# Decode attention beside a gated MLP on one core: weight matrices laid flat in 4.5 rows a partition, w_gate first, and half rows told apart in the sums over partitions

## The chip, the cores and the metric

The kernel runs on one core of a Trainium2 chip. The metric is the device time of one execution in microseconds (us), the median of several runs. All data are float32.

## The reference

One token is decoded: attention over a long cache, beside a gated MLP, both from the same normalised row x.

```python
D, H, Sk, Dh, Df = 576, 32, 16384, 128, 4608
xn = (x - mean(x)) / sqrt(var(x) + 1e-5)               # x: [576]
q  = (xn @ wq).reshape(H, Dh)                          # wq: [576, 4096]
s  = einsum("hd,hkd->hk", q, k_cache) * Dh**-0.5       # k_cache: [32, 16384, 128]
o  = einsum("hk,hkd->hd", softmax(s), v_cache)         # v_cache: [32, 16384, 128]
a  = o.reshape(4096) @ wo                              # wo: [4096, 576]
h  = gelu(xn @ w_gate) * (xn @ w_up)                   # both [576, 4608], gelu by tanh
out = x + a + h @ w_down                               # w_down: [4608, 576]
```

The caches are 537 MB of the 588 MB that are read; wq has 9.4 MB, w_gate and w_up 10.6 MB each.

## The kernel before

**What one head does.** The K cache of a head is one tile of 8.4 MB, 128 positions on each of 128 partitions, in two buffers that take turns (kb for even heads, ka for odd ones); V has one buffer, vt. DVE multiplies the whole K tile by q (qb, on every partition) and sums over the 128 features (L398, L402). TensorE and ScalarE make the softmax from that; TensorE multiplies the weights pe by V in 32 matmuls of 4 weight columns and 512 streamed columns (L386). Four of these stand in four different quarters of the array's columns. All large loads are issued on SP, one after the other, by an order written out by hand: before each, SP waits for a semaphore that says that the buffer is free.

**The three projections ahead of the heads.** `xn @ w` for wq, w_gate and w_up is made on DVE, because a row vector times a matrix needs every weight once. A matrix is laid with 4 of its first 512 rows on each partition (loads q0, q2 of wq, and so on), and the last 64 rows, cut into halves, make a tail with half a row on each partition (qt, gt, ut). `rows` scales each row on a partition by its element of xn (xp, xt) and adds them up: one tensor_scalar (L277) and scalar_tensor_tensor instructions (`add`, L266); the last ones write the tile both. What remains is the sum over the partitions. `sums` (L292 to L300) makes it on TensorE for each of the three matrices, with a weight tile of ones in 32 columns: the columns of both are cut into four quarters i and three banks b, and quarter i goes to the output partitions 32 i to 32 i + 31:

```python
m = g.matmul(pw[32 * i : 32 * i + 32, b, :SEL], ones[:, :32], bv[:, i, b * SEL : (b + 1) * SEL], start=True, stop=True)
```

`select` (L305 to L311) then turns the row of sums into a tile: a product with the mask m32 and a reduction on DVE. For q it makes qsel, from which TensorE and ScalarE make qb; for w_gate and w_up it makes gu (for w_up ScalarE and GpSimd do it). In the order on DVE, the select of a matrix stands between the rows of the next matrix, so that TensorE can sum meanwhile.

**What sets the order of the loads.** The buffers of the projections lie in the same memory as kb, ka and vt. wq and w_gate are loaded at once; w_up waits for the last row of wq; K of head 0 (two halves) for the last row of w_gate; K of head 1 for the third row of w_up (the semaphore value u_k); V of head 0 for the third sum (s_w, 3). After that each K load waits for s_kf (DVE is done with that buffer) and each V load for s_vf (TensorE is done with vt).

**The end.** w_down and wo are loaded last; DVE and TensorE share the sums of the last products.

Of the kernel before, what the change touches and what calls it, by code (L numbers as in the profile page):

```python
# [142 lines left out]
def plan(nc, pl, x, k_cache, v_cache, wq, wo, wg, wu, wd, out):  # L143
# [47 lines left out]
    qw, qt = [big("q0", 2 * HD, C + 8 * HD), big("q2", 2 * HD, C)], big("qt", HD // 2, C - 2 * HD)
    both = big("both", 12 * SEL, C + 8 * DF + 256)
    gw, gt = [big("g0", 2 * DF, B + 10240), big("g2", 2 * DF, A - 4 * DF)], big("gt", DF // 2, B)
    uw, ut = [big("u0", 2 * DF, A + 6 * DF), big("u2", 2 * DF, C)], big("ut", DF // 2, A + 4 * DF)
# [51 lines left out]
    k_xd = op("dve", lambda g: g.tensor_copy(xd, xn[:, DM:].unsqueeze(2).to_broadcast([1, D - DM, 2])), k_xn)
    xm = xn[:, :DM].rearrange("o (p j) -> o j p", j=DJ)
    for j in range(DJ):
        k = op("pe", lambda g, j=j: g.transpose(px[:, j : j + 1], xm[:, j, :], ones[:1, :1]), k_xn)
    k = op("pe", lambda g: g.transpose(px[:, DJ : DJ + 1], xd.rearrange("o d s -> o (d s)"), ones[:1, :1]), k_xd)  # L250
    k = op("dve", lambda g: g.tensor_copy(xp, px[:, : DJ + 1]), k)
    k_x = op("dve", lambda g: g.tensor_scalar(xt, par, xp[:, DJ:], None, op0=ALU.mult), k, c_par)
    c_h = op("dve", lambda g: g.tensor_copy(hcol[:, :H].rearrange("p (q r) -> p q r", q=4),
                                            ident.rearrange("p (q r) -> p q r", q=4)[:, :, : H // 4]), i1)
# [13 lines left out]
    def tails(s, t, d):  # L268
        n = t.shape[-1]
        for i in range(2):  # L270
            c = s[:, i * n : (i + 1) * n]
            add(c, t, xt[:, i : i + 1], c, d)

    def rows(w, t, d, parts, between=None):
        n = w[0].shape[-1] // 2
        r = [u[:, j * n : (j + 1) * n] for u in w for j in range(2)]
        op("dve", lambda g: g.tensor_scalar(r[0], r[0], xp[:, :1], None, op0=ALU.mult), d[0], k_x)  # L277
        add(r[1], r[1], xp[:, 1:2], r[0])
        made = between and between()
        for i in range(2):  # L280
            c = r[1][:, i * n // 2 : (i + 1) * n // 2]
            add(c, t, xt[:, i : i + 1], c, d[1])
        k_s = add(r[2], r[2], xp[:, 2:3], r[1], d[2])
        v = [u.rearrange("p (i c) -> p i c", i=4) for u in (r[3], r[2])]
        for lo, hi, to in parts:
            k = add(bv[:, :, to : to + hi - lo], v[0][:, :, lo:hi], xp[:, 3:4], v[1][:, :, lo:hi])
        pads = [op("pool", lambda g, lo=lo, hi=hi: g.memset(bv[:, :, lo:hi], 0.0), k_s)
                for lo, hi in ((384, SEL), (SEL + 384, 2 * SEL), (2 * SEL + 256, 3 * SEL)) if len(parts) > 1]
        pl.then("dve", [s_r], k, *pads[-1:])
        return k_s, k, made  # L290
# [13 lines left out]

    def select(dst, c, r, n):  # L305

        t = dst.shape[-1]
        v = sel[:, : 3 * c].rearrange("p (b r t) -> p b r t", b=3, t=t)
        m = m32[:, : 3 * c // t].rearrange("p (b r) -> p b r", b=3).unsqueeze(3).to_broadcast([P, 3, c // t, t])
        k = op("dve", lambda g: g.tensor_mul(v, pw[:, :, :c].rearrange("p b (r t) -> p b r t", t=t), m), (s_w, n), c_m32)  # L310
        return op("dve", lambda g: g.tensor_reduce(dst, sel[:, : r * t].rearrange("p (r t) -> p t r", r=r), axis=AX.X, op=ALU.add), k)  # L311
# [264 lines left out]
```

## Time and profile before

| | |
|---|---|
| median of 3 runs | 1361.17 us (1360.52 to 1361.29) |
| the profiled execution, its own time | 1361.59 us |
| its span, first to last instruction | 1360.3 us |
| DVE busy | 1243.2 us (91%) |
| TensorE matmuls busy (PE) | 389.3 us (29%) |
| ScalarE (ACT), GpSimd (POOL) busy | 66.8 and 35.9 us |
| read from HBM | 587.60 MB, 432 GB/s over the span |

Busy shares are means over the whole span. The head of the program, up to about 130 us, where the projections are made and the first heads are loaded, is told by the timeline and not by the shares. The trace shows each float32 matmul as two MATMULs, here called passes, so 12 matmuls of the program are 24 in it. Four passes that stand in different column quarters of the array overlap in time.

### The profile page before, as it was taken

What the parts mean: (1) busy time and instruction counts of PE and PEld (TensorE: products, weight loads), DVE (VectorE), ACT (ScalarE), POOL (GpSimd) and SP (SyncE); (2) the same over time, 40 slices, a digit from 0 to 9 for tenths busy, and PEclk for the clock granted to TensorE, in tenths of its full rate; (3) what the DMA queues carried; (4) which work ended last, traced back from release to release, by engine and by line L of the source; (5) the groups of instructions that cost most, each with busy time, mean ns of one, the idle gap of its engine ahead of it and who ended that gap; (6) DMA issues with size and microseconds to landing.
All of it is one profiled execution on the core that took longest, in us unless ns stands there. A gap on an engine that the chain in (4) does not pass through costs nothing. (4 is left out here: it accounts for less than half of the span.)

```text
span 1360.3 us, 6949 instructions
## 1 busy us (share of the span) xinstructions
PE 389.3 (29%) x2640; PEld 121.8 (9%) x2640; DVE 1243.2 (91%) x222; ACT 66.8 (5%) x234; POOL 35.9 (3%) x29
## 2 busy tenths in 40 slices
PE   0211233333221333333222333332223333322135
PEld 0000011011000111101000111000001111000011
DVE  7999999999988888899888888998888889988888
ACT  0000000000000000000000000000000000000000
POOL 0063000000000000000000000000000000000000
PEclk9655666666556666666556666665666666655667
DMA  9999999999999999999999999999999999999998
GB/s 404 429 438 432 432 432 432 447 443 436 432 432 432 432 432 432 432 432 432 443 447 436 432 432 432 432 432 432 432 432 432 437 453 436 432 432 432 431 428 378
DMA packets 12245, 587.62 MB, mean 432 GB/s; under 512 B 1362, under 2 KB 1618, under 8 KB 2132
## 3 DMA queue, kind: packets, MB, share of 16 engines
q1 hardware_dynamic: 12242, 587.60, 99.8%
q8 instruction: 1, 0.02, 0.0%
q10 hardware_dynamic: 2, 0.00, 0.0%
HBM read 587.60 MB, written 0.00 MB: 432 GB/s over the span
## 5 line engine op out<-in xcount | busy, mean ns | idle before, releaser
L386 PE MATMUL po<-vt,pe 128*4 128x512 f32 x2048 | 291.8, 733 | 605.7 <-PEq L130 605.7
L398 DVE TENSOR_TENSOR kb<-kb,qb 128x16384 f32<-128x16384 f32 (+1 forms) x17 | 277.3, 16314 | 31.9 <-DVEq L130 31.8
L398 DVE TENSOR_TENSOR ka<-ka,qb 128x16384 f32<-128x16384 f32 x16 | 275.6, 17225 | 31.4 <-DVEq L130 31.4
L402 DVE TENSOR_REDUCE sc<-kb 128x128 f32<-128x16384 f32 x16 | 275.5, 17220 | 2.3
L402 DVE TENSOR_REDUCE sc<-ka 128x128 f32<-128x16384 f32 x16 | 275.5, 17220 | 2.3
L386 PEld LDWEIGHTS po<-vt,pe 128*4 128x4 f32 x2048 | 56.4, 98 | 814.1 <-issue 814.1
L379 PE MATMUL pt<-ident,pm 128*1 128x128 f32 x32 | 11.9, 371 | 227.2 <-PEq L130 227.2
L437 ACT ACTIVATE o<-po 128x512 f32<-128x512 f32 x32 | 19.1, 597 | 871.4 <-ACTq L130 871.4
L391 PE MATMUL pc<-m,o 128*128 128x1 f32 x256 | 32.7, 249 | 28.9 <-PEq L130 28.9
L391 PEld LDWEIGHTS pc<-m,o 128*128 128x128 f32 x256 | 31.0, 191 | 57.8 <-issue 57.8
L266 DVE SCALAR_TENSOR_TENSOR wacc<-wd,hT,wacc 128x576 f32<-128x576 f32 x36 | 29.5, 819 | 4.1 <-DMA wd<-in_B_w_down_dram 2.9
L299 PE MATMUL pw<-both,ones 128*32 128x396 f32 x72 | 11.9, 826 | 62.5 <-PEq L130 62.5
L407 DVE TENSOR_REDUCE nm<-pt 1x1 f32<-1x128 f32 x32 | 8.9, 279 | 21.5 <-DVEq L130 21.5
L379 PEld LDWEIGHTS pt<-ident,pm 128*1 128x1 f32 x32 | 2.5, 79 | 232.4 <-issue 232.4
L381 PE MATMUL pb<-nm,ones 1*128 1x1 f32 x64 | 17.7, 343 | 18.5 <-PEq L130 18.5
L381 PEld LDWEIGHTS pb<-nm,ones 1*128 1x128 f32 x64 | 15.9, 306 | 27.9 <-issue 27.9
L433 ACT ACTIVATE nb<-pb 128x1 f32<-128x1 f32 x32 | 5.5, 172 | 258.3 <-ACTq L130 258.3
L405 DVE TENSOR_REDUCE pm<-sc 128x1 f32<-128x128 f32 x32 | 9.2, 286 | 7.6 <-DVEq L130 7.6
L377 PE MATMUL pqb<-qsel,hsel 128*128 128x128 f32 x64 | 15.3, 321 | 1.8 <-PEq L130 1.8
L435 ACT ACTIVATE pe<-sc,nb 128x128 f32<-128x128 f32 x32 | 12.8, 402 | 6.1 <-ACTq L130 6.1
L318 ACT ACTIVATE hsel<-hcol 128x128 f32 (+1 forms) x34 | 10.2, 301 | 40.5 <-DVE qsel L311 40.4
L340 POOL TENSOR_TENSOR tmp<-tmp 128x576 f32<-128x576 f32 (+3 forms) x4 | 11.3, 2835 | 0.3
(89 smaller groups left out, 173.7 us busy)
## 6 DMA issues: line engine op xcount, KB each, us to landing
g<-in_B_w_gate_dram SPq DMA_DIRECT2D x2, 4608.0 KB, 39.5
u<-in_B_w_up_dram SPq DMA_DIRECT2D x2, 4608.0 KB, 32.3
q<-in_A_wq_dram SPq DMA_DIRECT2D x2, 4096.0 KB, 17.4
kb<-in_A_k_cache_dram SPq DMA_DIRECT2D x2, 4096.0 KB, 25.8
wd<-in_B_w_down_dram SPq DMA_DIRECT2D x1, 8064.0 KB, 42.0
wo<-in_A_wo_dram SPq DMA_DIRECT2D x1, 3456.0 KB, 35.9
wd<-in_B_w_down_dram SPq DMA_DIRECT2D x1, 2304.0 KB, 28.1
wo<-in_A_wo_dram SPq DMA_DIRECT2D x1, 2304.0 KB, 40.9
```

Of the source, the lines that this page charges most:

```text
L266: return op("dve", lambda g: g.scalar_tensor_tensor(out, w, c, into, op0=ALU.mult, op1=ALU.add), *deps)
L299: m = g.matmul(pw[32 * i : 32 * i + 32, b, :SEL], ones[:, :32], bv[:, i, b * SEL : (b + 1) * SEL], start=True, stop=True)
L340: k = op("pool", lambda g, o=o, r=r: g.tensor_tensor(o, v[:, :r, :], v[:, r : 2 * r, :], op=ALU.add), k)
L377: g.matmul(pqb[:, 0, :DH], hsel, qsel, start=True, stop=True).then_inc(s_pq, 1)
L379: g.transpose(pt[:1, 0, :P], pm, ident).then_inc(s_pt, 1)
L381: g.matmul(pb[:, 0, :1], ones[:1, :], nm, start=True, stop=True).then_inc(s_pb, 1)
L386: m = g.matmul(po[q : q + 4, 0, :], pe[:, k : k + 4], vt[:, k * DH : (k + 4) * DH], start=k < 16, stop=k >= N - 16)
L391: m = g.matmul(pc[:, 0, :1], o4[:, j * DH : (j + 1) * DH], m32[:, j : j + 1], start=j == 0, stop=j == 3)
L398: g.tensor_mul(kd, kd, qb[i].unsqueeze(1).to_broadcast([P, n[1] - n[0], DH])).then_inc(s_d, 1)
L402: g.tensor_reduce(sc[i], kt[i].rearrange("p (n d) -> p n d", d=DH), axis=AX.X, op=ALU.add).then_inc(s_d, 1)
L435: g.activation(pe, sc[i], AF.Exp, bias=nb, scale=SCALE, accum_out=ls[:, bass.ds(h, 1)]).then_inc(s_p, 1)
L437: g.activation(o4, po[:, 0, :], AF.Copy).then_inc(s_o4, 1)
```

## The change

- The order of the matrices is w_gate, wq, w_up instead of wq, w_gate, w_up.
- Each matrix is laid flat: 1152 half rows, 9 on each partition (NK), all contiguous in HBM. There is no tail. A matrix comes in two loads: 5 and 4 half rows for w_gate, 4 and 5 for wq and w_up. Each matrix has one tile (g, q, u); u takes the place of g.
- `rows` goes by half rows. On an even partition the half rows with even k are first halves of a row, on an odd partition second halves. It keeps two running sums, one for even and one for odd k, and each writes half of both.
- So a sum over partitions must tell even partitions from odd ones. mk holds blocks of 32 columns, with ones on the even partitions, with ones on the odd ones, or with zeros, and each matmul now takes 128 weight columns out of it and adds into all 128 output partitions: four matmuls accumulate in each of three banks. Streamed columns are 384 instead of 396, and the padding of both is gone.
- xp gets 9 columns, made from a spread copy of xn (xd), five transposes and three DVE instructions.
- hcol, the mask m96 (for w_gate's select, which needs 12 columns a piece) and mk are made on POOL; po and acc are cleared on ACT instead of DVE.
- w_up waits for the last row of w_gate, K of head 0 for the last row of wq, K of head 1 for the last row of w_up. qb of head 0 is made after the second sum instead of the first.

```diff
-DJ = 4
-DM = P * DJ
+NK = 2 * D // P
-SEL = 396
+SEL = 384
...
     B, A, C = 0, SLOT, 2 * SLOT
...
+    AT = 2 * HD * NK
+    END = AT + 2 * DF * NK
+    qw, gw = big("q", HD * NK // 2, 0), big("g", DF * NK // 2, AT)
+    uw, both = big("u", DF * NK // 2, AT), big("both", 12 * SEL, END)
+    mk, m96 = big("mk", 256, END + 48 * SEL), big("m96", 96, END + 48 * SEL + 1024)
...
-    d_q = [dma("sp", qw[0], main["q"][:, : 2 * HD]), dma("sp", qt, tail["q"]), dma("sp", qw[1], main["q"][:, 2 * HD :])]
+    def halves(w):
+        return w.rearrange("d (s f) -> (d s) f", s=2).rearrange("(p k) f -> p (k f)", k=NK)
+
+    def load(t, w, first, *deps):
+        n = w.shape[-1] // 2
+        return [dma("sp", t[:, lo * n : hi * n], halves(w)[:, lo * n : hi * n], *deps) for lo, hi in ((0, first), (first, NK))]
+
+    d_g = load(gw, wg, 5)
     d_x = dma("act", xrow, xf)
-    d_g = [dma("sp", gw[0], main["g"][:, : 2 * DF]), dma("sp", gt, tail["g"]), dma("sp", gw[1], main["g"][:, 2 * DF :])]
+    d_q = load(qw, wq, 4)
...
+    c_h = op("pool", lambda g: g.tensor_copy(mk.rearrange("p (a s u) -> p a s u", a=2, s=2)[:, :, :, 32:],
+                                             par.unsqueeze(1).unsqueeze(3).to_broadcast([P, 2, 2, 32])), c_par)
...
-        op("dve", lambda g, z=z: g.memset(z, 0.0))
+        op("act", lambda g, z=z: g.activation(z, hcol[:, H : H + 1].unsqueeze(2).to_broadcast([P, z.shape[1], 512]), AF.Copy), c_z)
...
+    def rows(w, d, first, between=None):
+        n = w.shape[-1] // NK
+        r = [w[:, k * n : (k + 1) * n] for k in range(NK)]
+        done = []
+        for k in range(NK):
+            if k == first:
+                made = between and between()
+            c, dep = xp[:, k : k + 1], d[k >= first]
+            if k < 2:
+                done.append(op("dve", lambda g, k=k, c=c: g.tensor_scalar(r[k], r[k], c, None, op0=ALU.mult), dep, k_x))
+            elif k < NK - 2:
+                done.append(add(r[k % 2], r[k], c, r[k % 2], dep, done[k - 2]))
+            else:
+                v, old = (t.rearrange("p (i c) -> p i c", i=2) for t in (r[k], r[k % 2]))
+                done.append(add(bv[:, 2 * (k % 2) : 2 * (k % 2) + 2, : n // 2], v, c, old, dep, done[k - 2]))
+        pl.then("dve", [s_r], done[-1], c_h)
+        return done[-1], made
...
             for b in range(3):
-                for i in range(4):
-                    m = g.matmul(pw[32 * i : 32 * i + 32, b, :SEL], ones[:, :32], bv[:, i, b * SEL : (b + 1) * SEL], start=True, stop=True)
+                for i, at in enumerate((32, 0, 96, 64)):
+                    m = g.matmul(pw[:, b, :SEL], mk[:, at : at + P], bv[:, i, b * SEL : (b + 1) * SEL], start=i == 0, stop=i == 3)
             m.then_inc(s_w, 1)
...
-    _, q_k, _ = rows(qw, qt, d_q, [(384 * b, min(384 * b + 384, HD // 4), SEL * b) for b in range(3)])
-    d_u = [dma("sp", uw[0], main["u"][:, : 2 * DF], q_k), dma("sp", ut, tail["u"]), dma("sp", uw[1], main["u"][:, 2 * DF :])]
-    _, g_k, k = rows(gw, gt, d_g, [(0, DF // 4, 0)], lambda: select(qsel, 384, 8, 1))
+    g_k, _ = rows(gw, d_g, 5)
+    d_u = load(uw, wu, 4, g_k)
+    q_k, k_g = rows(qw, d_q, 4, lambda: select(gu[:, 0], m96, 12, 32, 1))
...
-    u_k, _, k_g = rows(uw, ut, d_u, [(0, DF // 4, 0)], lambda: select(gu[:, 0], SEL, 32, 2))
+    u_k, k = rows(uw, d_u, 4, lambda: select(qsel, m32[:, :9], DH, 8, 2))
...
-    dma("sp", kt[0][:, : N // 2 * DH], kv[0][:, : N // 2 * DH], g_k, sem=s_kh)
+    dma("sp", kt[0][:, : N // 2 * DH], kv[0][:, : N // 2 * DH], q_k, sem=s_kh)
```

On DVE, the last matrix (w_up) with the select that stands in it, before; a row is the line, the operation, out<-in and the shape:

```order
L277 TENSOR_SCALAR u_104<-u_104,xp 128x4608 [waits c_dve,d12]
L266 SCALAR_TENSOR_TENSOR u_104<-u_104,xp 128x4608 [waits c_dve]
L310 TENSOR_TENSOR tmp<-pw,m_59 128x1188 [waits c_dve,w]
L311 TENSOR_REDUCE gu<-tmp 128x36 [waits c_dve]
L266 SCALAR_TENSOR_TENSOR u_104<-ut,xt,u_104 128x2304 [waits c_dve,d13]
L266 SCALAR_TENSOR_TENSOR u_104<-ut,xt,u_104 128x2304 [waits c_dve]
L266 SCALAR_TENSOR_TENSOR u_105<-u_105,xp,u_104 128x4608 [waits c_dve,d14]
L266 SCALAR_TENSOR_TENSOR both<-u_105,xp 128x4x1152 [waits c_dve]
```

and the same place now:

```order
L287 TENSOR_SCALAR u<-u,xp 128x2304 [waits c_dve,d9]
L287 TENSOR_SCALAR u<-u,xp 128x2304 [waits c_dve]
L276 SCALAR_TENSOR_TENSOR u<-u,xp 128x2304 [waits c_dve] x2
L313 TENSOR_TENSOR tmp<-pw,m_59 128x1152 [waits c_dve,w]
L315 TENSOR_REDUCE qsel<-tmp 128x128 [waits c_dve]
L276 SCALAR_TENSOR_TENSOR u<-u,xp 128x2304 [waits c_dve,d10]
L276 SCALAR_TENSOR_TENSOR u<-u,xp 128x2304 [waits c_dve] x2
L276 SCALAR_TENSOR_TENSOR both<-u,xp 128x2304 [waits c_dve] x2
```

Four half rows now stand ahead of the select, which is that of q instead of that of w_gate; five half rows stand behind it, and K of head 1 is issued after the last of them instead of after the last but one.

On SP, the loads from the start up to w_up, before:

```order
L66 DMA q_97<-in_A_wq_dram 128x8192
L66 DMA qt<-in_A_wq_dram 128x2048
...
L66 DMA q_98<-in_A_wq_dram 128x8192
L66 DMA g_101<-in_B_w_gate_dram 128x9216
L66 DMA gt<-in_B_w_gate_dram 128x2304
L66 DMA g_102<-in_B_w_gate_dram 128x9216
L66 DMA u_104<-in_B_w_up_dram 128x9216 [waits c_dve]
```

and now:

```order
L65 DMA g<-in_B_w_gate_dram 128x11520
L65 DMA g<-in_B_w_gate_dram 128x9216
...
L65 DMA q<-in_A_wq_dram 128x8192
L65 DMA q<-in_A_wq_dram 128x10240
L65 DMA u<-in_B_w_up_dram 128x9216 [waits c_dve]
```

w_gate now stands first, and w_up is issued behind four loads instead of six (left out are the branches of the barrier, between the second load and the third).

## Rows read from the trace of the kernel before

**Rows 1.** The page: GB/s in 40 slices, and the queue of the loads.

```profile
GB/s 404 429 438 432 432 432 432 447 443 436 432 432 432 432 432 432 432 432 432 443 447 436 432 432 432 432 432 432 432 432 432 437 453 436 432 432 432 431 428 378
...
q1 hardware_dynamic: 12242, 587.60, 99.8%
```

**Rows 2.** Timeline (start, length, instruction, idle before): first load, and who waited for loads.

```profile
0.75 0.42 SPq L66 DMA_DIRECT2D q<-in_A_wq_dram  x1
...
12.92 2.35 DVE L277 TENSOR_SCALAR q<-q,xp 128x4096 f32<-128x4096 f32 x1 [2.13 <-DMA q<-in_A_wq_dram]
...
35.97 2.62 DVE L277 TENSOR_SCALAR g<-g,xp 128x4608 f32<-128x4608 f32 x1 [1.45 <-DMA g<-in_B_w_gate_dram]
...
132.45 9.01 PE L386 MATMUL po<-vt,pe 128*4 128x512 f32 x64 [3.66 <-PEq L130]
...
171.22 8.40 PE L386 MATMUL po<-vt,pe 128*4 128x512 f32 x64 [6.38 <-PEq L130]
```

**Rows 3.** Timeline: the issues of the first K loads, and DVE's start on head 0.

```profile
62.59 0.80 SPq L66 DMA_DIRECT2D kb<-in_A_k_cache_dram  x2
...
84.64 0.33 SPq L66 DMA_DIRECT2D ka<-in_A_k_cache_dram  x1
...
90.03 8.69 DVE L398 TENSOR_TENSOR kb<-kb,qb 128x8192 f32<-128x8192 f32 x1 [0.37 <-DVEq L130]
...
127.03 0.34 SPq L461 DMA_DIRECT2D kb<-in_A_k_cache_dram  x1
```

**Rows 4.** Groups by form, 0 to 130 us: count, busy us, mean ns, idle before.

```profile
L266 DVE SCALAR_TENSOR_TENSOR g<-gt,xt,g 128x2304 f32<-128x2304 f32 x2 | 5.2, 2618 | 0.1
...
L266 DVE SCALAR_TENSOR_TENSOR q<-qt,xt,q 128x2048 f32<-128x2048 f32 x2 | 4.7, 2351 | 0.1
...
L277 DVE TENSOR_SCALAR g<-g,xp 128x4608 f32<-128x4608 f32 x1 | 2.6, 2621 | 1.4 <-DMA g<-in_B_w_gate_dram 1.4
...
L277 DVE TENSOR_SCALAR q<-q,xp 128x4096 f32<-128x4096 f32 x1 | 2.4, 2353 | 2.1 <-DMA q<-in_A_wq_dram 2.1
L311 DVE TENSOR_REDUCE gu<-tmp 128x36 f32<-128x1152 f32 x1 | 2.2, 2166 | 0.0
L311 DVE TENSOR_REDUCE qsel<-tmp 128x128 f32<-128x1024 f32 x1 | 1.9, 1871 | 0.0
...
L310 DVE TENSOR_TENSOR tmp<-pw,m 128x1152 f32<-128x1152 f32 x1 | 1.4, 1358 | 0.1
```

**Rows 5.** Timeline of PE and its weight loads: a sum, and a burst of L386.

```profile
62.77 4.19 PE L299 MATMUL pw<-both,ones 128*32 128x396 f32 x24 [14.50 <-PEq L130]
63.40 0.23 PEld L299 LDWEIGHTS pw<-both,ones 128*32 128x32 f32 x4 [0.43 <-issue]
64.06 0.23 PEld L299 LDWEIGHTS pw<-both,ones 128*32 128x32 f32 x4 [0.43 <-issue]
...
137.42 0.10 PEld L386 LDWEIGHTS po<-vt,pe 128*4 128x4 f32 x4 [0.33 <-issue]
137.85 0.10 PEld L386 LDWEIGHTS po<-vt,pe 128*4 128x4 f32 x4 [0.33 <-issue]
```

**Rows 6.** The group of L386 on the page; its longest and shortest burst (timeline).

```profile
L386 PE MATMUL po<-vt,pe 128*4 128x512 f32 x2048 | 291.8, 733 | 605.7 <-PEq L130 605.7
...
1021.37 9.98 PE L386 MATMUL po<-vt,pe 128*4 128x512 f32 x64 [21.03 <-PEq L130]
...
1137.32 8.34 PE L386 MATMUL po<-vt,pe 128*4 128x512 f32 x64 [21.12 <-PEq L130]
```

**Rows 7.** Windows: stretch, length, busy of PE, PEld, DVE, ACT, POOL, PEclk, DMA.

```profile
63.00:64.00 1.00, 1.00 (x8) 0.23 (x4) 1.00 (x1) 0.00 (x0) 0.00 (x0) 0.50 0.26 111
...
138.00:139.00 1.00, 1.00 (x16) 0.20 (x8) 1.00 (x1) 0.00 (x0) 0.00 (x0) 1.00 1.66 721
```

**Rows 8.** Timeline: 128x128 matmuls of two passes, their weight loads and lengths.

```profile
47.46 0.50 PEld L295 LDWEIGHTS pqb<-qsel,hsel 128*128 128x128 f32 x2 [9.91 <-issue]
47.49 0.77 PE L295 MATMUL pqb<-qsel,hsel 128*128 128x128 f32 x2 [9.22 <-PEq L130]
...
143.22 0.30 PEld L377 LDWEIGHTS pqb<-qsel,hsel 128*128 128x128 f32 x2
```

More of the change, by code (lines that the diff above doesn't have):

```diff
@@ L170, in plan @@
     xrow, eps = small("xrow", [1, D]), small("eps", [P, 1])
-    m32, m4, par = small("m32", [P, 33]), small("m4", [P, 4]), small("par", [P, 2])
+    m32, m4, par = small("m32", [P, 32]), small("m4", [P, 4]), small("par", [P, 2])
     st = small("st", [1, 2, nc.vector.BN_STATS_DIM])
     mv, std, rstd = small("mv", [1, nc.vector.BN_AGGR_DIM]), small("std", [1, 1]), small("rstd", [1, 1])
-    xp, xt = small("xp", [P, DJ + 1]), small("xt", [P, 2])
+    xp, xt = small("xp", [P, NK]), small("xt", [P, NK // 2])
     qsel, hsel, hcol = small("qsel", [P, DH]), small("hsel", [P, P]), small("hcol", [P, H + 4])
@@ L183, in plan @@
     over = place["tmp"]
-    xn, xd = small("xn", [1, D], over), small("xd", [1, D - DM, 2], over + 4 * D)
+    xn = small("xn", [1, D], over)
     t1, th, t2 = (small(f"t{i}", [P, FT]) for i in range(3))
@@ L190, in plan @@
     B, A, C = 0, SLOT, 2 * SLOT
[L191 to L194, printed above, removed]
+    AT = 2 * HD * NK
[3 more added lines that the diff above has]
+    mk, m96 = big("mk", 256, END + 48 * SEL), big("m96", 96, END + 48 * SEL + 1024)
+    xd = big("xd", P * 5, END + 48 * SEL + 2048)[:1]
     kt = [big("kb", N * DH, B), big("ka", N * DH, A)]
@@ L228, in plan @@
     i0 = op("pool", lambda g: g.memset(ident, 0.0))
-    for t, c in ((ones, 1.0), (eps, EPS), (hcol, 0.0), (m32[:, 32:], 0.0)):
-        op("pool", lambda g, t=t, c=c: g.memset(t, c))
+    for t, c in ((ones, 1.0), (eps, EPS), (mk, 0.0), (hcol, 0.0)):
+        c_z = op("pool", lambda g, t=t, c=c: g.memset(t, c))
     i1 = op("pool", lambda g: g.affine_select(out=ident, in_=ident, compare_op=ALU.not_equal, fill=1.0, base=0,
@@ L245, in plan @@
     k_xn = op("dve", lambda g: g.tensor_scalar(xn, xrow, mv[:, 0:1], rstd, op0=ALU.subtract, op1=ALU.mult), k)
[L246 to L254, printed above, removed]
+    pairs = bass.AP(xn.tensor, xn.offset, [list(xn.ap[0]), [1, 5], [NK, P // 2], [4, 2]])
+    k = op("dve", lambda g: g.tensor_copy(xd.rearrange("o (a m s) -> o a m s", a=5, s=2), pairs), k_xn)
+    for a in range(5):
+        k_t = op("pe", lambda g, a=a: g.transpose(px[:, a : a + 1], xd[:, a * P : (a + 1) * P], ones[:1, :1]), k)
+    op("dve", lambda g: g.tensor_copy(xp[:, 0:NK:2], px[:, :5]), k_t)
+    k = op("dve", lambda g: g.tensor_scalar(xt, px[:, 1:5], par[:, 1:2], None, op0=ALU.mult), c_par)
+    k_x = op("dve", lambda g: g.scalar_tensor_tensor(xp[:, 1:NK:2], px[:, :4], par[:, :1], xt, op0=ALU.mult, op1=ALU.add), k)
     for z in (po, acc):
-        op("dve", lambda g, z=z: g.memset(z, 0.0))
+        op("act", lambda g, z=z: g.activation(z, hcol[:, H : H + 1].unsqueeze(2).to_broadcast([P, z.shape[1], 512]), AF.Copy), c_z)
     bv = both.rearrange("p (i c) -> p i c", i=4)
@@ L262, in plan @@
     op("pool", lambda g: g.memset(qsel, 0.0))
-    op("pool", lambda g: g.memset(hsel, 0.0), sig=s_h0)
+    k = op("pool", lambda g: g.memset(hsel, 0.0))
+    pl.then("pool", [s_h0, s_h0], k)
     def add(out, w, c, into, *deps):
         return op("dve", lambda g: g.scalar_tensor_tensor(out, w, c, into, op0=ALU.mult, op1=ALU.add), *deps)
[L268 to L290, printed above, removed]
+    def rows(w, d, first, between=None):
[15 more added lines that the diff above has]
+        return done[-1], made
     def sums(g):
@@ L303, in plan, with select @@
     hint("pe")
[L305 to L311, printed above, removed]
-    _, q_k, _ = rows(qw, qt, d_q, [(384 * b, min(384 * b + 384, HD // 4), SEL * b) for b in range(3)])
-    d_u = [dma("sp", uw[0], main["u"][:, : 2 * DF], q_k), dma("sp", ut, tail["u"]), dma("sp", uw[1], main["u"][:, 2 * DF :])]
-    _, g_k, k = rows(gw, gt, d_g, [(0, DF // 4, 0)], lambda: select(qsel, 384, 8, 1))
+    def select(dst, mask, t, r, n):
+        v = sel.rearrange("p (b r t) -> p b r t", b=3, t=t)
+        m = mask.rearrange("p (b r) -> p b r", b=3).unsqueeze(3).to_broadcast([P, 3, SEL // t, t])
+        k = op("dve", lambda g: g.tensor_mul(v, pw[:, :, :SEL].rearrange("p b (r t) -> p b r t", t=t), m), (s_w, n), c_m32, c_h)
+        n = dst.shape[-1]
+        return op("dve", lambda g: g.tensor_reduce(dst, sel[:, : r * n].rearrange("p (r t) -> p t r", r=r), axis=AX.X, op=ALU.add), k)
+    g_k, _ = rows(gw, d_g, 5)
+    d_u = load(uw, wu, 4, g_k)
+    q_k, k_g = rows(qw, d_q, 4, lambda: select(gu[:, 0], m96, 12, 32, 1))
     def pick(g, h):
         return g.activation(hsel, hcol[:, bass.ds(h, 1)].to_broadcast([P, P]), AF.Copy)
+    u_k, k = rows(uw, d_u, 4, lambda: select(qsel, m32[:, :9], DH, 8, 2))
     op("act", lambda g: pick(g, 0), k, c_h, sig=s_h0)
-    k = op("act", lambda g: g.activation(qb[0], pqb[:, 0, :DH], AF.Copy), (s_q0, 2))
-    pl.then("act", [s_qb, s_h0], k)
-    u_k, _, k_g = rows(uw, ut, d_u, [(0, DF // 4, 0)], lambda: select(gu[:, 0], SEL, 32, 2))
+    k = op("act", lambda g: g.activation(qb[0], pqb[:, 0, :DH], AF.Copy), (s_q0, 3))
+    pl.then("act", [s_qb], k)
     g_, u_ = gu[:, 0], gu[:, 1]
@@ L335, in plan @@
     op("act", lambda g: pick(g, 1), (s_q0, 3), sig=s_hs)
-    v = sel[:, : 32 * FT].rearrange("p (r t) -> p r t", r=32)
-    k = op("pool", lambda g: g.tensor_mul(v, v, m32[:, :32].unsqueeze(2).to_broadcast([P, 32, FT])), k, c_m32)
+    v = sel.rearrange("p (r t) -> p r t", r=32)
+    k = op("pool", lambda g: g.tensor_mul(v, v, m32.unsqueeze(2).to_broadcast([P, 32, FT])), k, c_m32)
     for r in (16, 8, 4, 2, 1):
```

7 lines of the change are left out of this document (4 added, 3 removed).

## Prediction

> **What bounds the kernel now.** I read the page's line of DMA rates first. Every slice after the first stands at 429 to 453 GB/s until the last two, and the one queue that carries the loads is busy 99.8% of the span [rows 1]. The total of 587.6 MB does not change, so the time is the start of the first load, the bytes at this rate, any stretch in which the queue is empty, and the tail.
>
> The second view is the timeline, taken at the instructions that waited for a load. The first wq load (4.194 MB) lets DVE start at 12.92 us, the first w_gate load (14.156 MB counted from the start) at 35.97, the first V (55.83 MB) lets PE start at 132.45, and the second V (72.61 MB) at 171.22 [rows 2]. The slopes are 2.314, 2.315 and 2.310 us per MB. So the landing of byte number M is 3.21 + 2.314 M, and had the queue been dry between 35.97 and 132.45, the middle slope would stand out. At the steady slope of 2.310 those 41.67 MB would take at most 0.2 us less. **No change of the head of the program can win more than a few tenths of a microsecond** unless the slope or the 3.21 changes, and 0.2% of this kernel, 2.7 us, is about what a measurement tells from no change. What can happen is a loss: a load that is issued too late. Then every microsecond of empty queue is lost, because nothing later has slack in DMA.
>
> So the question is the SP issues. Before, K of head 1 (tile ka) is issued at 84.64 [rows 3]. The bytes ahead of it (39.06 MB) land at 93.6 by the line. A load that finds the queue empty lands 3.21 - 0.75 = 2.46 us after its issue plus its bytes [rows 2]. To follow without a gap, ka must be issued by 93.6 - 2.46 = 91.1. Before, that left 6.5 us.
>
> **The change part by part.** Start: the first two loads are still issued ahead of the barrier, so 3.21 stays. The loads have longer rows; the slope was the same for rows of 8, 32 and 64 KB, so nothing is taken for that, and 0.3 us either way is kept. The preparation of xp (a copy of 640 elements on one partition, five transposes, three small DVE instructions) replaces like work that was done by 12.92 [rows 2], while the first load, now 5.9 MB, lands at 16.9; the new copies on POOL and the clearing of po and acc on ACT lie under that load too. All at nothing: 4 us of cover at least.
>
> DVE: a half row costs less than half a row plus the tail costs. From [rows 4], a tensor_scalar takes 2.62 us for 4608 elements and 2.35 for 4096, so 1.42 for 2304 and 1.28 for 2048 (estimates from these two); the fused multiply-add takes 2.62 for 2304 and 2.35 for 2048 as measured on the old tails. With 0.035 us between instructions, which the same rows show beside their starts, w_gate or w_up costs 2 x 1.455 + 7 x 2.655 = 21.5 us and wq 2 x 1.315 + 7 x 2.385 = 19.3.
>
> PE: the sums of one matrix were 12 matmuls of 32 weight columns and 396 streamed columns, in the trace 24 passes (two for each float32 matmul) of which four run side by side; a round of four took 0.66 us and the whole 4.19 [rows 5]. Now each matmul fills all 128 weight columns, so the 24 passes of 384 columns follow one another: 9216 columns in a row. The nearest row is the P times V burst of a head: 64 passes of 512 columns, four side by side, so 8192 columns in a row. Its 32 bursts take 9.12 us in the mean, and 8.34 and 9.98 are the ends [rows 6]. [...] I take the burst plus 1024 columns at the fast rate, 0.86 us: **S = 10.0 us for one sum instead of 4.2, from 9.2 to 10.9.** [...]
>
> Was that hidden before, and is it now? Before, DVE had other rows to do while PE summed. Now, walked along DVE:
> - w_gate: first load 16.9, five halves to 27.7, second load (10.62 MB) lands 27.8, four halves to 38.4. w_up is issued there; it would be needed by 49.6 - 2.46 = 47.1: hidden by 8.7 us.
> - First sums from 38.6 to 38.6 + S. DVE does four halves of wq until 45.9 and then stands at the select for w_gate until 38.7 + S, 2.8 us with S = 10.0. The select is 1.36 + 2.17 [rows 4] and gaps, 3.6. Then five halves of wq, 11.9: done at 54.2 + S = 64.2. K of head 0 is issued there; needed by 74.2 - 2.46 = 71.7: hidden by 7.5.
> - Second sums from 64.4 to 64.4 + S. Four halves of w_up until 72.6, wait to 74.5, select of q 1.36 + 1.87 and gaps, 3.3, five halves 13.3 (the second w_up load landed at 74.2): done at 71.15 + 2S = 91.15. **ka is issued at 91.2, where 91.1 is the limit.** The slack of 6.5 us is spent.
> - Third sums end near 101.3 and release the first V, needed by 110.5: hidden by 9. DVE begins head 0 at 91.4 instead of 90.03, so kb is free and K of head 2 issued near 128.4 instead of 127.03 [rows 3]; needed by 132.4 - 2.46 = 129.9: 1.5 us remain, and a late ka moves both alike.
>
> The sum: empty queue = max(0, S1 + S2 - 19.9). With both at the mean of the bursts it is 0.1 us, with both at the slow end 1.8, with one high and one low 0 to 0.3; the DVE estimates add some 0.7 either way. I take +0.3. The tail has the same instructions. On the profiled execution (span 1360.3, own time 1361.59) this is a span of 1360.6; on the median, 1361.17 + 0.3 = **1361.5**.
>
> **The rivals.** (a) Weight loads in line, the slow side. A full 128-column load of weights takes 0.25 us at the slow clock and 0.15 at the fast one (0.50 and 0.30 for two) [rows 8]. If each of the 24 passes has to wait for its own, S rises by at least 24 x 0.15 = 3.6 to 13.6, and the empty queue is 27.2 - 19.9 = 7.3: 1368.5. It decides from S of about 11.3 on, where the loss passes 2.7 us. For it: no row of before streams long passes through full-width weights. Against it: four 32-column loads have as many columns, take 0.23 us, and lie wholly inside a 0.66 round [rows 5], and the two full loads at 47.46 follow each other in 0.50 us without a gap although a pass of 128 columns lies between them [rows 8]. [...]
>
> [...]
>
> (c) Faster, by fewer loads: six weight loads in place of nine. If each load cost its start of 2.46 us by itself, three fewer would give 7.4 us back: 1353.8. Against it: between 12.92 and 35.97 lie three loads and the slope is that of the big ones [rows 2]; queued loads overlap their starts. [...]
>
> (d) The change does less than it says: all of ka's lateness is covered because the sums are shorter than S or DVE quicker. That is my own forecast without the 0.3 and cannot be told apart by time.
>
> **How the numbers follow.** Forecast with (d), within 0.2% (1358.4 to 1363.9): 0.80. (a), or a smaller part of it, or DVE a few microseconds later than walked: 0.13. (b): 0.04. (c): 0.03. So slower 0.17, same 0.80, faster 0.03. The forecast's own range is 1360.6 to 1363.3. For 8 in 10 the range runs from 1360.3 to 1365.0, into the smaller cases of (a).
>
> **What would show it.** Sums of 9.2 to 10.9 us on PE with passes 0.64 us apart at first and 0.32 later; two DVE waits of 2 to 3 us ahead of the selects; ka issued at 90 to 93; the first V's matmuls starting at 132.4 to 134, since any empty queue shows there as a shift; GB/s of the third slice near 432 or a little lower. Wrong would be: sums over 11.5 us, ka issued after 94, a first V after 135.2, or a first V before 132.

## The result and the profile after

The changed kernel takes 1363.06 us, the kernel before 1360.84 beside it: a ratio of 1.0015, 95% interval 1.0009 to 1.0021. That is 2.2 us more, inside the 0.2% that the prediction called no change, and 1.6 above its 1361.5. One of the 22 executions took 1797.64 us, in a slower state, and is left out of the ratio. The profiled execution has a span of 1361.9 (1360.3 before) and an own time of 1363.18.

The page's rates and the load queue, to set beside [rows 1]: the first slice is the same, and what is missing is spread over a few others.

```profile
GB/s 404 434 428 431 433 429 435 431 431 449 435 435 433 431 431 431 435 431 431 445 439 435 433 431 431 431 435 431 431 443 441 435 433 431 431 431 433 433 441 364
...
q1 hardware_dynamic: 11810, 587.60, 99.7%
```

The timeline of the changed kernel: the issues of w_up (u) and of K of head 0 (kb), the first two sums on PE, the two selects on DVE with their waits, the issue of K of head 1 (ka), the first and the last burst on V (start, length, instruction, idle before).

```profile
38.62 0.81 SPq L65 DMA_DIRECT2D u<-in_B_w_up_dram  x2
...
38.83 10.93 PE L303 MATMUL pw<-both,mk 128*128 128x384 f32 x24 [28.37 <-PEq L129]
...
49.80 1.36 DVE L313 TENSOR_TENSOR tmp<-pw,m 128x1152 f32<-128x1152 f32 x1 [3.64 <-PE pw L303]
...
65.42 0.80 SPq L65 DMA_DIRECT2D kb<-in_A_k_cache_dram  x2
...
65.59 9.51 PE L303 MATMUL pw<-both,mk 128*128 128x384 f32 x24 [15.61 <-PEq L129]
...
75.14 1.36 DVE L313 TENSOR_TENSOR tmp<-pw,m 128x1152 f32<-128x1152 f32 x1 [1.42 <-PE pw L303]
...
91.77 0.33 SPq L65 DMA_DIRECT2D ka<-in_A_k_cache_dram  x1
...
134.52 9.93 PE L389 MATMUL po<-vt,pe 128*4 128x512 f32 x64 [4.96 <-PEq L129]
...
1332.35 8.35 PE L389 MATMUL po<-vt,pe 128*4 128x512 f32 x64 [20.79 <-PEq L129]
```

The last burst on V in the kernel before:

```profile
1330.17 9.19 PE L386 MATMUL po<-vt,pe 128*4 128x512 f32 x64 [20.73 <-PEq L130]
```

The sums last 10.93 and 9.51 us, DVE waits 3.64 and 1.42 us for them, and ka is issued at 91.77 instead of 84.64 [rows 3]. The first V starts PE at 134.52, against 132.45 [rows 2]: 2.07 us late. The last V starts it at 1332.35, against 1330.17 before: 2.18 late. **So all of the loss is made before 135 us and is carried to the last V nearly unchanged.** (The spans differ by 1.6 only: behind its last V the profiled execution of the kernel before took 0.6 us more than that of the changed kernel.) How much of it is the late ka, the DMA issues tell (KB for equal ones, us from issue to landing); before, and then after:

```profile
ka<-in_A_k_cache_dram SPq DMA_DIRECT2D x1, 28.3
```

```profile
ka<-in_A_k_cache_dram SPq DMA_DIRECT2D x1, 23.3
```

Before, ka lands at 84.64 + 28.3 = 112.9, after at 91.77 + 23.3 = 115.1. The bytes take 19.4 us at 2.314 us per MB, so this load, issued when the queue was about to run out, needed 3.9 us on top of its bytes and not the 2.46 that I had read from the first load.

What these 3.9 us are is seen at the end of a load. Each ends with 16 packets under 512 B, by their number one from each of the 16 DMA engines. The first eight of ka's 16 lie in 111 to 112.32 us before and in 111 to 113.01 after:

```profile
DMA packets 16, 0.52 MB, mean 397 GB/s; under 512 B 8, under 2 KB 8, under 8 KB 8
```

```profile
DMA packets 19, 0.72 MB, mean 359 GB/s; under 512 B 8, under 2 KB 8, under 8 KB 8
```

So the middle engines are 0.7 us late, which is what the prediction's 2.46 gives for this issue (91.77 - 91.1). The last engine does not follow that sum: its packet starts at 114.74, against 112.56 before, 2.2 late. The same is seen at V. The DMA lines of two stretches, 131.0 to 133.3 and 133.3 to 135.0, in the changed kernel:

```profile
DMA packets 30, 1.05 MB, mean 456 GB/s; under 512 B 14, under 2 KB 14, under 8 KB 14
```

```profile
DMA packets 15, 0.85 MB, mean 501 GB/s; under 512 B 2, under 2 KB 2, under 8 KB 2
```

In the kernel before, all 16 lie in the first stretch. After, 14 engines end V by 133.2, and two more between 133.3 and 135.0. V has landed when the last engine has: its end packet ends at 134.08 and PE starts at 134.52, 0.44 us later (131.98 and 132.45 in the kernel before, 0.47). In the stretches 1328 to 1331 and 1331 to 1332.5, at the last V, the counts are again 14 and 2. The packets do not name their engine, but the distance from the first to the last of the 16 is 1.9 us at ka and stays at 1.7 to 1.9 at every load up to the last V, so the reading is that two engines that fell behind near 94 us are behind for the whole kernel.

```profile
DMA packets 44, 0.79 MB, mean 263 GB/s; under 512 B 14, under 2 KB 14, under 8 KB 14
```

```profile
DMA packets 32, 0.55 MB, mean 369 GB/s; under 512 B 2, under 2 KB 2, under 8 KB 2
```

### The profile page after: what moved, and what is told of

It reads as the page before. It is cut to its first block, busy times and chain, and to the rows that moved or that the text cites. A ratio compares the mean times of both kernels' runs of the same rounds, so it can differ in the third digit from the quotient of the medians.

```text
span 1361.9 us, 6951 instructions
## 1 busy us (share of the span) xinstructions
PE 408.1 (30%) x2640; PEld 134.3 (10%) x2640; DVE 1235.9 (91%) x227; ACT 68.4 (5%) x236; POOL 25.7 (2%) x29
## 3 DMA queue, kind: packets, MB, share of 16 engines
q1 hardware_dynamic: 11810, 587.60, 99.7%
## 5 line engine op out<-in xcount | busy, mean ns | idle before, releaser
L303 PE MATMUL pw<-both,mk 128*128 128x384 f32 x72 | 30.4, 591 | 56.3 <-PEq L129 56.3
L303 PEld LDWEIGHTS pw<-both,mk 128*128 128x128 f32 x72 | 16.6, 236 | 69.0 <-issue 62.9
L384 PE MATMUL pb<-nm,ones 1*128 1x1 f32 x64 | 17.7, 343 | 18.5 <-PEq L129 18.5
L384 PEld LDWEIGHTS pb<-nm,ones 1*128 1x128 f32 x64 | 15.9, 306 | 27.9 <-issue 27.9
L276 DVE SCALAR_TENSOR_TENSOR g<-g,xp 128x2304 f32<-128x2304 f32 x5 | 13.1, 2619 | 0.2
```

The lines of the kernel that those rows point to most:

```text
L303: m = g.matmul(pw[:, b, :SEL], mk[:, at : at + P], bv[:, i, b * SEL : (b + 1) * SEL], start=i == 0, stop=i == 3)
L384: g.matmul(pb[:, 0, :1], ones[:1, :], nm, start=True, stop=True).then_inc(s_pb, 1)
```

## The experiments

Theory L: the loss is the late ka, and it is late because the serial sums and the wait for w_up's last row stand in the chain to it. Rival F: the flat loads or the masks cost by themselves. Five kernels stem from the changed one (e1 to e5), six from the kernel before (f1 to f6), without flat loads.

**e1: ka in two halves, the upper one issued two DVE instructions earlier.** Left out below are the semaphore of the upper half and DVE's wait for it.

```diff
...
-    load_k(1, u_k)
+    dma("sp", kt[1][:, N // 2 * DH :], kv[1][:, N // 2 * DH :], u_k[6], sem=s_kg)
+    dma("sp", kt[1][:, : N // 2 * DH], kv[1][:, : N // 2 * DH], u_k[-1], sem=s_k[1])
...
```

> The changed kernel, but K of head 1 (ka) is loaded in two halves: the upper half, whose memory holds only w_up half rows that are read by then, two DVE instructions earlier (near 86.5 us), the lower half where the whole load stood (near 91.8). Theory L (the loss is the late ka, issued into an emptied queue): the queue never empties, the first V lands as in the kernel before (PE starts on it near 132.4 instead of 134.5), time 1360.9 +- 0.4. Rival F (the flat loads or the new masks cost by themselves, wherever ka is issued): V still near 134.5, time near 1363.

Measured: 1361.04 us, ratio 1.0002 (0.9993 to 1.0011). The timeline shows the first half issued at 86.14 (the two issues are merged in one row) and V on time:

```profile
86.14 5.64 SPq L65 DMA_DIRECT2D ka<-in_A_k_cache_dram  x2
...
132.40 9.07 PE L389 MATMUL po<-vt,pe 128*4 128x512 f32 x64 [3.16 <-PEq L129]
```

Everything else of the change is in this kernel, flat loads, masks and serial sums, and the loss is gone. Rival F falls.

**e2: every sum twice.**

```diff
-            for b in range(3):
+            for b in (0, 1, 2, 0, 1, 2):
```

> The changed kernel with the 12 matmuls of each sum done twice, with the same results. Each sum lasts 24 x 0.32 = 7.7 us longer. Theory L: both lie in the chain to ka, so ka is issued 15.4 us later (107.2), and since the queue is already empty there, all of it is lost: 1363.1 + 15.4 = 1378.5 +- 1.5. Rival F: the sums have cover left and the time rises by a few us at most, below 1370.

Measured: 1378.75 us, ratio 1.0129 (1.0114 to 1.0145). ka goes to 107.69 and the first V to 149.57:

```profile
72.86 18.15 PE L303 MATMUL pw<-both,mk 128*128 128x384 f32 x48 [15.61 <-PEq L129]
...
107.69 0.33 SPq L65 DMA_DIRECT2D ka<-in_A_k_cache_dram  x1
...
149.57 8.66 PE L389 MATMUL po<-vt,pe 128*4 128x512 f32 x64 [4.10 <-PEq L129]
```

ka is issued 15.9 us later than in the changed kernel and lands 14.4 us later, since it now finds an idle queue; the first V starts 15.05 us later than there and the time is 15.7 us longer. Past the limit the chain through the sums costs about one for one.

**e3: half of the passes.**

```diff
-                for i, at in enumerate((32, 0, 96, 64)):
+                for i, at in enumerate((32, 0)):
-                    m = g.matmul(pw[:, b, :SEL], mk[:, at : at + P], bv[:, i, b * SEL : (b + 1) * SEL], start=i == 0, stop=i == 3)
+                    m = g.matmul(pw[:, b, :SEL], mk[:, at : at + P], bv[:, i, b * SEL : (b + 1) * SEL], start=i == 0, stop=i == 1)
```

> The changed kernel with two of the four matmuls of each bank left out (half of the sum over the columns is not computed), so 12 passes instead of 24. Theory L: a sum lasts 5.5 to 6.5 us, less than the four half rows beside it, DVE doesn't wait at the selects, ka is issued near 86.7, before the queue empties: first V at 132.4, time 1360.9 +- 0.4. Rival F: the loads and masks are as in the changed kernel, so 1363.

Measured: 1361.01 us, ratio 1.0 (0.9991 to 1.0009). The second sum takes 6.89 us (5.5 to 6.5 expected), DVE's four half rows cover it, ka goes out at 87.50, V is on time:

```profile
62.09 6.89 PE L303 MATMUL pw<-both,mk 128*128 128x384 f32 x12 [16.44 <-PEq L129]
...
87.50 0.33 SPq L65 DMA_DIRECT2D ka<-in_A_k_cache_dram  x1
...
132.34 8.83 PE L389 MATMUL po<-vt,pe 128*4 128x512 f32 x64 [5.47 <-PEq L129]
```

e1 and e3 take away either link of the chain, and either is enough.

**e4: the clock raised ahead of the sums**, by four matmuls whose result nobody reads, released when DVE has three half rows left.

```diff
...
+            take(g, s_up)
+            for _ in range(4):
+                g.matmul(fin[:, 0, :], ident, bass.AP(hcol.tensor, hcol.offset, [list(hcol.ap[0]), [0, 512]]), start=True, stop=True)
             take(g, s_r)
...
+            if k == 6:
+                pl.then("dve", [s_up], done[-1], c_h)
```

> The changed kernel with four matmuls of 512 columns, whose result nobody reads, ahead of each sum: PE starts them when DVE has three half rows left, so that the sums find the clock risen. Theory L with the clock as its cause: a sum lasts 7.9 to 8.5 us instead of 9.5 to 10.9, ka is issued at 87 to 88.5, time 1360.9 +- 0.4. If the clock falls again before a sum starts, or isn't raised, sums stay at 9.5 to 11 and the time near 1363.

Measured: 1362.62 us, ratio 1.0011 (1.0002 to 1.002): half a miss. The sums and ka are as expected, the time is not. Timeline, and the queues of the load page:

```profile
62.84 7.98 PE L308 MATMUL pw<-both,mk 128*128 128x384 f32 x24 [1.89 <-PEq L129]
...
87.90 0.33 SPq L65 DMA_DIRECT2D ka<-in_A_k_cache_dram  x1
...
132.92 9.31 PE L394 MATMUL po<-vt,pe 128*4 128x512 f32 x64 [7.50 <-PEq L129]
...
172.02 8.53 PE L394 MATMUL po<-vt,pe 128*4 128x512 f32 x64 [10.55 <-PEq L129]
```

```profile
q1 hardware_dynamic: 11810, 587.60, 99.7%
q8 instruction: 1, 0.02, 0.0%
q14 instruction: 1, 0.01, 0.0%
```

A sum of 7.98 us, 24 passes at 0.33, has each pass at about the 0.32 us of the late passes in the changed kernel's sums; the granted clock of 63 to 70 us is 1.00. ka at 87.90 is only 0.4 us later than in e3, and yet V is 0.5 us late and the second V 0.8 (172.02 against 171.22 [rows 2]). Among the packets of 84 to 86 us stands one of the queue q14, and of 138 to 140 us one of q8: instructions that are fetched among the loads. The 16 end packets of the load then running spread from 0.66 to 1.21 us with the first fetch and from 1.21 to 1.65 with the second: each time one engine drops behind.

**e5: the same as a loop of one matmul**, so that the program of PE is shorter.

```diff
-            for _ in range(4):
+            with g.Fori(0, 4):
                 g.matmul(fin[:, 0, :], ident, ...
```

> As e4 (four unread matmuls ahead of each sum), but written as a loop of one matmul on PE, so that PE's program is not longer by three matmuls. In e4 the queue never ran empty and yet the first V came 0.5 us late and the second 0.8: its profile shows two instruction packets among the loads (8 KB at 84.7, 16 KB at 138.9), each beside one of the 16 DMA engines falling behind for good. If those fetches are the cause, and the shorter program has none in these places: ka again near 88, sums near 8 us, first V at 132.4, time 1360.9 +- 0.4. If the unread matmuls themselves slow the loads: near 1362.6 as e4.

Measured: 1363.18 us, ratio 1.0015 (1.0006 to 1.0024). The time did not come down, so the expectation failed as it was put. In the trace the packet of q14 is still there at 84 to 86 us and V is 0.5 us late as in e4; none of q8 lies near 139, and the second V's lateness falls from 0.8 to 0.3:

```profile
132.91 9.14 PE L394 MATMUL po<-vt,pe 128*4 128x512 f32 x64 [7.45 <-PEq L129]
...
171.52 8.61 PE L394 MATMUL po<-vt,pe 128*4 128x512 f32 x64 [10.02 <-PEq L129]
```

The spans of all executions tell more: their median is 1360.0 for e5 and 1361.2 for e4, against 1359.6 for the kernel before beside each. Outside the span e5 spends 3.2 us in the median, where the kernel before and e4 have 1.3. So inside the span e5 wins back most of e4's loss, and most of its own loss lies outside; what fills that time isn't shown by the trace. So the second fall of V in e4 goes with the second fetch; that the fetches are the cause of both is only read from the trace, and the times of e4 and e5 stay unexplained in part.

**f1, f5, f2, f3: the kernel before, with nothing but ka issued later**: behind the last row of w_up, behind two short ScalarE copies after it, behind the first bank of the last sum, and behind the whole of it.

```diff
-    load_k(1, u_k)
+    load_k(1, u_l)
+    load_k(1, u_a)
+    load_k(1, u_k, (s_e, 3))
+    load_k(1, u_k, (s_w, 3))
```

One of the four new lines stands in each kernel, in this order. u_l is the last row of w_up, u_a the second of two copies of ones to pe on ScalarE that wait for u_l, s_e a semaphore that counts up after bank 0 of each sum.

> The kernel before, with ka (K of head 1) waiting for the last row of w_up instead of the last but one: issued at 89.7 instead of 84.6. No flat loads, no new masks. If a load into an emptied queue lands 2.46 us plus its bytes after its issue (as in my prediction), the limit is 91.1 and nothing is lost: 1360.9. If it lands 3.9 us plus its bytes after (23.3 us in all, as the changed kernel's ka did), the limit is 89.65 and the loss is 0 to 0.3: 1360.9 to 1361.2.

> The kernel before, with ka waiting for two short ScalarE copies behind the last row of w_up: issued near 90.4, between f1 (89.86, nothing lost) and f2 (91.48, 2.5 us lost). If the loss sets in when the first of the 16 DMA engines runs dry (their last packets of the load ahead end within 0.4 us of each other), and then costs the whole uneven restart, it is 0 to 0.3 at 90.4: 1361.0 to 1361.3. If the loss grows evenly with lateness from 89.65 on, it is about 0.8 to 1.2: 1361.8 to 1362.3.

> The kernel before, with ka waiting until a third of the last sum is done, near 91.4, which is nearly where the changed kernel issues it (91.77). With 2.46 us: 0.3 us late, 1361.2. With 3.9 us: 1.75 late, 1362.6. If the flat loads were the cause of the changed kernel's loss, the time stays at 1360.9.

> The kernel before, with ka waiting for the whole last sum: issued at 94.1. With 2.46 us: 3.0 late, 1363.9. With 3.9 us: 4.5 late, 1365.3. If lateness costs nothing: 1360.9.

The rows of the four in this order: the issue of ka, and its us to landing.

```profile
89.86 0.33 SPq L66 DMA_DIRECT2D ka<-in_A_k_cache_dram  x1
...
ka<-in_A_k_cache_dram SPq DMA_DIRECT2D x1, 23.3
```

```profile
90.33 0.33 SPq L66 DMA_DIRECT2D ka<-in_A_k_cache_dram  x1
...
ka<-in_A_k_cache_dram SPq DMA_DIRECT2D x1, 23.8
```

```profile
91.48 0.33 SPq L66 DMA_DIRECT2D ka<-in_A_k_cache_dram  x1
...
ka<-in_A_k_cache_dram SPq DMA_DIRECT2D x1, 23.7
```

```profile
93.63 0.33 SPq L66 DMA_DIRECT2D ka<-in_A_k_cache_dram  x1
...
ka<-in_A_k_cache_dram SPq DMA_DIRECT2D x1, 21.7
```

Issue plus that figure is the landing; a landing of 112.9 is on time:

| kernel | ka issued | landed | late | time, us | kernel before beside it |
|---|---|---|---|---|---|
| f1 | 89.86 | 113.2 | 0.3 | 1361.26 (1.0001, 0.9992 to 1.0010) | 1361.07 |
| f5 | 90.33 | 114.1 | 1.2 | 1362.27 (1.0009, 1.0000 to 1.0018) | 1360.96 |
| f2 | 91.48 | 115.2 | 2.3 | 1363.55 (1.0020, 1.0011 to 1.0029) | 1361.07 |
| the changed kernel | 91.77 | 115.1 | 2.2 | 1363.06 (1.0015, 1.0009 to 1.0021) | 1360.84 |
| f3 | 93.63 | 115.3 | 2.4 | 1364.31 (1.0025, 1.0016 to 1.0035) | 1361.07 |
| e2 | 107.69 | 129.5 | 16.6 | 1378.75 (1.0129, 1.0114 to 1.0145) | 1361.03 |

Against the expectations: f1 does not tell 2.46 from 3.9 us within its interval. f5 fits an even growth of the loss (1361.8 to 1362.3). f2 rules out the 1361.2 of 2.46 us and lies 0.9 above the 1362.6 of 3.9 us, and f3 lies between its two figures, nearer to that of 2.46 us (1363.9). So neither start cost fits all four.

f2 has none of the change and ka at nearly the changed kernel's time: the same landing and nearly the same loss, 2.5 us against 2.2. And the price of lateness is not a straight line. From 89.86 to 91.48 the landing moves by 2.0 us, from there to 93.63 by 0.1, though ka goes out 2.2 us later; the time rises by 0.8 there, within the two intervals. f3 needs 21.7 - 19.4 = 2.3 us on top of its bytes, f2 4.3. In f3, where the queue had run empty on all engines, all of them end V in one stretch; in f2 they do not. The line of 133.3 to 135.0 in f3, and of f2 in the same stretch:

```profile
DMA packets 32, 1.05 MB, mean 617 GB/s; under 512 B 16, under 2 KB 16, under 8 KB 16
```

```profile
DMA packets 14, 0.72 MB, mean 424 GB/s; under 512 B 3, under 2 KB 3, under 8 KB 3
```

In f3 all 16 engines end V in this stretch and none before; in f2, 13 end earlier and three here, as two do in the changed kernel. The first 16 packets of ka in the traces, by their number one from each engine, show how it comes about. In the kernel before they start between 92.76 and 93.13 us, just as the load ahead ends. In f5 the last starts at 93.81. In the changed kernel 14 start by 93.75 and two at 94.3, and in f2 they start one by one from 92.69 to 94.82. In f3 all engines are idle by then; they start between 94.59 and 95.58 and end that packet within 0.5 us of one another. So where the load arrived while the engines were running out (f5, the changed kernel, f2), they started it at different times, and in the changed kernel they kept the difference. Why one engine takes up to 2 us longer than another isn't shown.

**f4: the kernel before with serial sums alone.**

```diff
-    sel = small("tmp", [P, 3 * SEL])
+    sel, mk = small("tmp", [P, 3 * SEL]), small("mk", [P, 224], place["o4"])
...
-    for t, c in ((ones, 1.0), (eps, EPS), (hcol, 0.0), (m32[:, 32:], 0.0)):
+    for t, c in ((ones, 1.0), (eps, EPS), (mk, 0.0), (mk[:, 96:128], 1.0), (hcol, 0.0), (m32[:, 32:], 0.0)):
...
-                    m = g.matmul(pw[32 * i : 32 * i + 32, b, :SEL], ones[:, :32], bv[:, i, b * SEL : (b + 1) * SEL], start=True, stop=True)
+                    m = g.matmul(pw[:, b, :SEL], mk[:, 96 - 32 * i : 224 - 32 * i], bv[:, i, b * SEL : (b + 1) * SEL], start=i == 0, stop=i == 3)
```

> The kernel before with one part of the change alone: each sum matmul takes 128 weight columns (ones in 32 of them, zeros elsewhere) and four accumulate, so that the 24 passes run one after another; loads, order and rows are those of before. A sum lasts 9.5 to 11 us instead of 4.2. DVE waits about 1 us at the first select and 2.5 at the second, so ka is issued near 88.2 instead of 84.6, still ahead of the limit (89.65 or 91.1): nothing lost, 1360.9 +- 0.4. If serial sums alone were the cause: near 1363.

Measured: 1363.15 us, ratio 1.0015 (1.0006 to 1.0024): a miss. ka still has its early place, and the loss is made at another load, K of head 2 (kb), which waits for DVE:

```profile
64.33 11.13 PE L299 MATMUL pw<-both,mk 128*128 128x396 f32 x24 [14.81 <-PEq L130]
...
75.49 1.40 DVE L310 TENSOR_TENSOR tmp<-pw,m 128x1188 f32<-128x1188 f32 x1 [3.54 <-PE pw L299]
...
89.64 0.33 SPq L66 DMA_DIRECT2D ka<-in_A_k_cache_dram  x1
...
130.45 0.34 SPq L461 DMA_DIRECT2D kb<-in_A_k_cache_dram  x1
...
172.59 7.86 PE L386 MATMUL po<-vt,pe 128*4 128x512 f32 x56 [4.33 <-PEq L130]
```

By the walk of the prediction kb's limit is 129.9; it went out at 130.45, and the second V came 1.4 us late. One engine is again the last: 15 of kb's 16 end packets lie before 152.7 us, one behind. The first V was not late: all 16 of its end packets lie before 131.7, as against 132.0 in the kernel before. PE starts on it at 133.49, for its weights pe come late from the softmax.

**f6: f4 without head 0's first half product** on DVE, so that kb comes free 8.7 us earlier.

```diff
-        products(g, 0, (0, N // 2))
```

> f4 (the kernel before with serial full-width sums) with one thing left out: for the first half of head 0's K tile DVE does not multiply by q (8.7 us; head 0's scores are then not the reference's). ka and the first V are issued as in f4 (89.6 and 106.1), but K of head 2, which waits for DVE, comes 8.7 us earlier, near 121.7 instead of 130.45. If the loss of f4 (1363.15) is the late K of head 2, the second V lands as in the kernel before (171.2) and the time is 1361.0 +- 0.4. If it is ka at 89.64 or the sums themselves: 1363 again.

Measured: 1360.83 us, ratio 1.0001 (0.9992 to 1.0010), with kb at 121.17 and the second V at 170.94:

```profile
121.17 0.34 SPq L460 DMA_DIRECT2D kb<-in_A_k_cache_dram  x1
...
170.94 9.05 PE L386 MATMUL po<-vt,pe 128*4 128x512 f32 x64 [11.96 <-PEq L130]
```

ka goes out at 88.92 here, 0.7 us earlier than in f4, but f4's first V had landed on time with its later ka. So f4 lost at kb. Serial sums were harmless to the load queue here only where every load that DVE releases had the slack for them.

## Why the prediction was right, and where it was off

The call, no change within 0.2%, held, with the time 1.6 us above the forecast and inside the range. The band of 0.2% is wide enough to hold a loss seven times the 0.3 us that was forecast, so the call alone does not show that the sum was right. Point by point:

- **What bounds the kernel** held. No run came out faster than the kernel before by more than its interval, and the losses are those of loads issued too late, but for e4 and e5, which are not wholly explained.
- **DVE's work** held. The walk gave w_gate done at 38.4, wq at 64.2, w_up at 91.15; the issues of the loads behind them stand at 38.62, 65.42 and 91.77. Of the 0.6 us of the last one 0.2 are there behind w_gate already, and the rest is the first sum, 10.93 instead of 10.0, less the second, 9.51. The waits at the selects were forecast at 2 to 3 us and took 3.64 and 1.42, for the same reason.
- **S** held: 10.93, 9.51 and 9.98 us for the three sums, inside or at the edge of 9.2 to 10.9. Rival (a) fell. Two of the three old sums took 4.19 us, at 0.66 a round throughout; the first took 3.52 and ended faster. The 0.86 us for 1024 columns in S were shown by no run as such: they are twice the 0.43 us that 512 columns took late in a burst [rows 5], at a granted clock of 1.00 [rows 7]. In the third sum 384 columns took 0.64 us at a granted clock of 0.50 (92 to 93 us) and 0.32 at 1.00 (96 to 97 us). The two full weight loads of [rows 8] took 0.50 us at a granted clock of 0.50 (47 to 48 us) and 0.30 at 1.00 (143 to 144). The weight loads of the first sum (start, length) are 0.64 us apart and then 14 of them take 4.42 us, 0.32 each: the 384 columns at 1.67 ns, as in the old sums (0.66 for 396), and at some 0.82 ns, near the late burst's 0.84 (0.43 for 512) [rows 5], with nothing for loads of 0.34 us and less.

```profile
40.88 0.34 PEld L303 LDWEIGHTS pw<-both,mk 128*128 128x128 f32 x1 [0.30 <-issue]
41.52 0.34 PEld L303 LDWEIGHTS pw<-both,mk 128*128 128x128 f32 x1 [0.30 <-issue]
...
44.08 0.34 PEld L303 LDWEIGHTS pw<-both,mk 128*128 128x128 f32 x1 [0.30 <-issue]
44.72 4.42 PEld L303 LDWEIGHTS pw<-both,mk 128*128 128x128 f32 x14 [0.30 <-issue]
```

  So full-width float32 weight loads were hidden here. A sum at 0.64 a pass throughout, the 0.04 of (b), did not come: with the same rows the passes turn to 0.32.
- **The limit of ka and the price of missing it** is the step that failed. "ka must be issued by 93.6 - 2.46 = 91.1" took the 2.46 us of the very first load, which starts 16 idle engines, for a load that meets them as they run out. There the runs show 3.9 (the changed kernel) and 4.3 (f2), so the limit stands between 89.86, where the landing is 0.3 late and the time equal within its interval (f1), and 90.33, where the landing is 1.2 late (f5). With 3.9, taken from that same landing, the sum is 91.77 + 3.9 + 19.4 - 112.9 = 2.2 us, which is what the median shows; f2, without the change, bears it out. The formula max(0, S1 + S2 - 19.9) should have read 18.5. The mechanism was right. Its term of empty queue was forecast at 0.3 us, would be 0.7 with the issue as measured, and was 2.2. What failed in it is the assumption that a load lands as one piece: 0.7 us is the lateness of the middle engines, 2.2 that of the last one, for which the landing waits. The sign "first V at 132.4 to 134" was missed by the same step, with 134.52.
- Rival (c) fell: six loads in place of nine gave nothing. The first slice is 404 GB/s in both kernels, and e1 and e3, with the same six loads, take the time of the kernel before.
- **kb at 1.5 us from its limit** was noted in the prediction and left out of f4's expectation: f4 shows that this second thin place alone can cost as much as ka. In the changed kernel kb went out at 127.80 and kept its slack.

## What to carry to other kernels

In this kernel, bound by one queue of loads (99.7% busy), an edit ahead of a load was worth what it did to the issue time of that load: nothing while slack remained (e1, e3), and 15.7 us for 15.9 of lateness past it (e2). So write a limit beside each load, bytes ahead of it over the rate, less some 4 us for its start (3.9 and 4.3 here), and look at the load with the least slack first, and at the next one after it. Where a buffer is freed piece by piece, issuing the first half of the load early is worth a try: in e1 it bought back the slack (1361.04 us against 1363.06) without touching the work that used it up.

## What the runs showed of the hardware that was not expected

- A load that came as the queue ran out was dearer, measured from its issue, than one that came 2 us later, or 16, into an idle queue: 4.3 us on top of its bytes (f2) against 2.3 (f3) and 2.4 (e2, 21.8 - 19.4).
- The 16 DMA engines don't catch up with one another here. By the distance of their first and last end packet, 1.9 us at 113 and 1.8 at 1330, two that were behind the others at the first V of the changed kernel are behind at the last one, 1200 us later, and the landing of the load is theirs.
- An instruction fetch among the loads (8 KB in e4 and e5, 16 KB in e4 and in e2 at 153.2 us) went each time with one more engine falling behind, by 0.4 to 0.6 us at its end packets, while no load was late. That the fetch holds up one DMA engine is the likely reading; it was not tried by itself.
- The granted clock in the windows can't be read at the start of these two programs. In the stretch 41 to 42 us of the changed kernel the column PEclk (after the five busy times) reads 1.00, and the passes of that stretch are 0.64 us apart, the rate that goes with 0.50 elsewhere (0.66 us for 396 columns [rows 5, 7], and 0.64 for 384 in the third sum). The trace's records of the clock begin only at 44.79 us here, at 1.00, where the passes turn to 0.32, and at 37.46 in the kernel before, at the end of its first sum; the column counts the time ahead of the first record as 1.00. There the rate is to be read from the passes.

```profile
41.00:42.00 1.00, 1.00 (x3) 0.56 (x2) 0.96 (x2) 0.00 (x0) 0.00 (x0) 1.00 1.51 655
```
